# Attention and two expert layers on one core: other goals for the attention steps, another order of the first loads, later copies, GpSimd in program order

## The chip, the cores and the metric

The kernel runs on one core of a Trainium2 chip. The core has a matrix engine (TensorE, PE in the profile), a vector engine (VectorE, DVE), a scalar engine (ScalarE, ACT), a general engine (GpSimd, POOL) and an engine that does nothing here but issue transfers (SyncE, SP). Each engine takes its own instructions in order and waits for others at semaphores. Transfers (DMAs) are issued from SP, ScalarE or GpSimd and run on 16 DMA engines of the core. The metric is the time of one execution on the device in microseconds.

## The reference, cut to what matters

Shapes: 4 batches, 8 heads, 576 positions, head width 64; this makes 2304 tokens of width 512.

```python
# 1. attention with a decay per position, causal
scores = q @ k.T / 8 + cum[i] - cum[j]         # cum = cumsum(log(clip(f, 1e-4, 1)))
x = softmax(scores, causal) @ v                # then heads side by side: [2304, 512]
# 2. first layer: dense, 512 -> 2048 -> 512
h = x @ w_in
x = (h * clip(h + 3, 0, 6) / 6) @ w_out
# 3. second layer: each token goes to one of 8 experts, 512 -> 1024 -> 512
e = argmax(x @ w_gate)
out = softmax(x @ w_gate)[e] * sigmoid(x @ w_output_gate)[e] * (relu(x @ w1[e]) @ w2[e])
```

## The kernel before

All products are made from pairs of 16-bit numbers: each float32 matrix is split into a high part (float16) and a low part, and three matmuls stand for one.

**Opening.** The attention of the first batch runs ahead alone, while the weights of the first layer come in and are split. The function `attn_seq` (L635 on) is a generator that hands out attention in steps. Its prologue loads pieces of q and k (`load(i, "kq")`) and of v, computes the cumulative decay on VectorE (`decay`), stores it to DRAM (`store_decay`, L153) and reads it back in rows into K (`load_cum`, L215). The first two pieces of q and k are transposed on TensorE; their copies into the other half of K and Q are made on GpSimd (L249). Three steps end in the prologue; then each entry of a written list, `plan`, is one step: a unit of attention ("q" or "t": scores of a head, softmax, and the product with v of a unit some places back), a preparation of a piece of q and k ("p") or of v ("v"). Later pieces are transposed by DMA, and `copy_rows` copies the transposed rows to a second place (L260 on GpSimd for pieces 0 to 3, L262 on ScalarE for later ones). The copy is put into the order of instructions when the count that it starts with (`COPY_LAG`) has run out, one off at each unit, or when a unit needs it (`flush_for`).

Units wait in a list, `pend`, and `LAG = 4` of them are held back between scores and product. When the last unit of a group of row blocks has had its product, the group waits for two counts (`XLAG`), one at each unit, and then its rows are transposed into `xT` by DMA (`xtrans`, L561) and the group is `complete`. Preparations neither push a unit nor count. There are 12 groups, three for each batch; `ends[i]` is the place in the plan of the last unit of group i.

**Steps of the opening.** `pre_step` takes one attention step, then handles the weights: at the steps in `PRE_CONV` one piece of w_in is converted (three VectorE instructions L760 to L764, the high part on ScalarE L769, the low part on GpSimd L770), and one further piece of weights is loaded from SP (`load_next(nc.sync)`, L746). The prologue has loaded five pieces from ScalarE's queue already. The opening ends when the groups that chunk 0 needs are complete, and two more steps follow.

**Main part.** The first layer runs over 6 chunks of 384 tokens. `moe1_steps(c)` has 32 steps for a chunk: 16 of x @ w_in (12 matmuls each, L803) and 16 of 12 matmuls of g @ w_out (L828). Between them attention steps are put in by pace: the loop has a goal for the chunk, `goals[c]`, a number of attention steps, and takes steps so that the goal is reached at 0.9 of the chunk's steps (0.75 in chunk 4). After the chunk's last step, a loop takes attention steps one after another until the groups that the next chunk needs are complete. When all of attention is done, `open_weights` gives its memory to the expert weights, whose loads and conversions are then spread over the following steps.

**What sets the order.** TensorE, ScalarE and VectorE run in program order in the opening and the main part (`manual_schedule`), SP in the opening's first part only. Elsewhere SP and GpSimd are ordered by a planner, which simulates the program and issues what it takes to be ready first. `issue_after` puts instructions behind a given one on its engine; `gate` holds the transposes into `xT` of the third block of the first batch.

The parts that the change touches, with the line numbers of the profile:

Of the kernel before, what the change touches and what calls it, by code (L numbers as in the profile page):

```python
# [33 lines left out]

GATE_LOAD = 8

COPY_LAG = 1

LEAD = 2

LAG = 4

XLAG = 2
# [19 lines left out]
def attention_moe_kernel(ctx: ExitStack, tc: tile.TileContext, q, k, v, f, w_in, w_out,  # L63
# [7 lines left out]
    NTB = 5  # L71
# [184 lines left out]
    def copy_rows(i, out, in_):  # L256

        def go():
            if i < SPARE_PIECES:
                nc.gpsimd.tensor_copy(out=out, in_=in_)  # L260
            else:
                nc.scalar.activation(out=out, in_=in_, func=AF.Copy)  # L262
        copies.append([COPY_LAG, i, go])

    def flush_copies(due):
        for x in [x for x in copies if due(x)]:
# [368 lines left out]
    def attn_seq():  # L635

        def drain(n):
            while len(pend) > (min(n, EARLY_LAG) if pend and first_units(pend[0]) else n):
                pv(pend.pop(0))

        def step(u):
            todo, behind[:] = behind[:], []
            for f_ in todo:
                f_()
            if u:
                flush_for(u)
                score(u)
            turns, unturned[:] = unturned[:], []
            while unsoft:
                soft(unsoft.pop(0))  # L650
            for x in turns:
                turn(x)
            while outs:
                outs.pop(0)()
            if u:
                unsoft.append(u)
                pend.append(u)

        def after(n):
            drain(n)  # L660
            finish(1)
            for x in copies:
                x[0] -= 1
            flush_copies(lambda x: x[0] < 0)

        unsoft = []
        setup_ident()
        cp = decay()
        nc.scalar.activation(out=ap1.tile([P, 4], F32, tag="nm", name="warm", bufs=4)[:, 0:1], in_=bias3, func=AF.Exp)
        for i in range(4):  # L670
            load(i, "kq")
        for i in range(2):
            load(i, "v")
        setup()
        store_decay(cp)
        for hh in range(2):
            load_cum(0, hh)
        load(2, "v")
        banks.extend([(ps_mm, "mm")] * 3 + [(ps_sc, "sc")] * 2 + [(ps_pv, "pv")] * 2 + [(ps_mm, "mm")])
        for i in range(PE_PIECES):  # L680
            prep_k(i)
            load_next(nc.scalar)
            prep_q(i)
            load_next(nc.scalar)
        while behind:
            behind.pop(0)()
        prep(0, 2, "k")
        load_next(nc.scalar)
        yield "end"
        prep_v(0, 0)  # L690
        yield "end"
        prep(0, 2, "q")
        prep_v(0, 1)
        yield "end"
        for it in plan:
            if it is None:
                step(None)
                after(LAG)
            elif it[0] == "p":
                if it[2] == 4 or it[2] < 2 and it[1]:  # L700
                    load_cum(it[1], min(it[2], 2))
                if it[1:] == (0, 3):
                    for _ in range(3):
                        load_ahead()
                prep(it[1], it[2])
            elif it[0] == "v":
                prep_v(it[1], it[2])
            else:
                step(it)
                yield "mid"  # L710
                after(LAG)
            yield "end"
        step(None)
        for n in range(LAG, -1, -1):
            after(n)
            yield "end"
            step(None)
        while late:
            finish(1)
            yield "end"  # L720
# [484 lines left out]
        if loads and (loads[0][0] == "wi" or nsteps[0] >= WO_STEP) and len(loads) > 2 * NF - EARLY_LOADS:  # L1205
            load_next(nc.sync)

    with tc.manual_schedule(engines={mybir.EngineType.SP}):
        while len(complete) < need[0]:
            pre_step()  # L1210
    for _ in range(LEAD):
# [1 line left out]
    held = False  # L1213
    EARLY_CONV_DONE = 2 * NF - len(conv)
    assert len(conv) == len(CONV_AT), (len(conv), nsteps)
    goals = [ends[need[c + 1] - 1] + 1 + LAG + XLAG for c in range(NCH - 1)]
    mp2 = None
    px_ctx = ctx.enter_context(ExitStack())
    iota = None
# [17 lines left out]
    for c in range(NCH):  # L1237
# [14 lines left out]
        for part in moe1_steps(c):  # L1252
            k_ += part == "end"
            now = k_ + (part == "mid")
            share = min(1.0, now / pace)
            if c == 0:
                share = F1_SHARE * now / NF if now < NF else F1_SHARE + (1 - F1_SHARE) * min(1.0, (now - NF) / (pace - NF))
            want = start + (goal - start) * share
            if part == "mid":
                held = nsteps[0] < want and adv_part() == "mid"  # L1260
                continue
            if held:
                adv_part()
                held = False
            while nsteps[0] < want and adv():
                pass
            for split in late_steps:
                split()
                load_next(nc.scalar)
            late_steps.clear()  # L1270
            for lo in wlo:
                lo()
            wlo.clear()
            if c == 0 and k_ == GATE_LOAD:
                load_gates()
            if conv and k_ == CONV_AT[2 * NF - EARLY_CONV_DONE - len(conv)]:
                assert conv[0] not in loads
                late_steps.append(conv_raw(*conv.pop(0), later=True))
            elif not conv and mp2 is None:
                stage_ctx.close()  # L1280
                mp2 = moe1_ctx.enter_context(tc.tile_pool(name="mp2", bufs=1))
                ps_x = px_ctx.enter_context(tc.tile_pool(name="ps_x", bufs=1, space=PSUM))
                setup_gates()
            if gq and k_ in (3, 4, 6, 7, 8, 9):
                run(gq[0])
                if k_ == 9:
                    gq.pop(0)
            if c == NCH - 2 and wp is None and len(complete) == 3 * B:
                open_weights()
            if wg_ and nw < 4 * KD + 1 and (c < NCH - 1 or k_ % 4 == 0 or k_ > NF and k_ % 4 != 1):  # L1290
                run(wg_)
                nw += 1
            if c == NCH - 1 and k_ > 14:
                for i in [rq.pop(0) for _ in range(min(2, len(rq)))]:
                    rank_onehot(R0, i, 0, P)
                    rank_onehot(R, i, P, CAP)
                    if i == NBL - 1:
                        reserve()
                        table(R0, 0, const, ps_mm, (0,), NBL)
                        for e in range(2):  # L1300
                            row = wi[:, 0, 2 * e]
                            gather(e, (0,), (row[:, 0:2 * DM].rearrange("p (a b) -> p a b", b=P),
                                                   row[:, 2 * DM:4 * DM]))
                            h_tile(e, (0,), wi[:, 0, 2 * e + 1].rearrange("p (a c b) -> p a c b", c=2, b=P))
# [123 lines left out]
```

## Time and profile before

| | us |
|---|---|
| median of 3 runs (lowest to highest) | 887.76 (887.01 to 891.34) |
| the profiled execution | 883.18 |
| its span in the profile | 881.5 |
| PE busy | 733.6 |
| ACT, DVE, POOL busy | 456.8, 454.1, 317.4 |

A profile comes from one execution. The page sums up each engine; a view of stretches gives the busy time of each engine between two moments; a view in order of time gives single instructions, with the idle time of their engine before them and what ended it. The granted clock of TensorE has two levels here, 1.2 and 2.4 GHz, shown as 0.5 and 1.0.

### The profile page before, as it was taken

The page shows a single profiled execution, that of the slowest core. Times are in us where ns is not written, and L with a number is a line of the kernel's source. Part 1 is how long each engine was busy: PE and PEld are TensorE (multiplying, and loading weights), DVE is VectorE, ACT ScalarE, POOL GpSimd, SP SyncE. Part 2 cuts the span into 40 slices and gives each one's busy share as a digit, 9 for nine tenths or more (in the row PEclk, how much of TensorE's full clock was granted, in tenths as well). Part 3 has the DMA queues.
Part 4 walks back from the last instruction along what each step waited for, and adds up shares of the span by engine and source line. Part 5 has one row for each costly group of instructions (what it writes and reads, how often), then busy time and mean ns, then how long its engine had stood idle before and what let it go on. Part 6 is the DMA issues. An engine that isn't in the chain of part 4 may idle for free. (4 is left out here: it accounts for less than half of the span.)

```text
span 881.5 us, 16560 instructions
## 1 busy us (share of the span) xinstructions
PE 733.6 (83%) x6142; PEld 481.3 (55%) x6153; DVE 454.1 (52%) x1254; ACT 456.8 (52%) x904; POOL 317.4 (36%) x402
## 2 busy tenths in 40 slices
PE   2456879749998499959896699969989999999994
PEld 2344546425565266626564366646567776666762
DVE  7687688635743065217642285127853456646520
ACT  5557577645765377327774376125442445545430
POOL 9566446562344334323454234110103421321010
PEclk7576899988999699969998799989999999999997
DMA  9994559984466846355685434250688679989300
GB/s 249 253 252 90 119 85 209 231 168 91 71 130 106 169 82 118 64 110 107 101 156 125 95 65 92 26 162 29 211 219 203 176 233 324 295 190 251 139 36 26
DMA packets 268066, 129.00 MB, mean 146 GB/s; under 512 B 218946, under 2 KB 251810, under 8 KB 267972
## 3 DMA queue, kind: packets, MB, share of 16 engines
q1 hardware_dynamic: 254564, 103.66, 54.2%
q0 software_dynamic: 4960, 15.73, 5.2%
q10 hardware_dynamic: 8448, 8.39, 3.1%
q8 instruction: 54, 0.88, 0.4%
q14 instruction: 40, 0.33, 0.1%
HBM read 71.52 MB, written 10.08 MB: 93 GB/s over the span
## 5 line engine op out<-in xcount | busy, mean ns | idle before, releaser
L803 PE MATMUL mm<-xT,wi 128*128 128x384 f16 x912 | 169.8, 344 | 60.4 <-DMA xT<-xn 55.9
L828 PE MATMUL mm<-g,wo 128*128 128x384 f16 (+1 forms) x1152 | 195.2, 328 | 0.3 <-POOL wo L770 0.3
L803 PEld LDWEIGHTS <-wi 128*128 128x128 f16 (+1 forms) x1152 | 113.3, 101 | 137.6 <-DMA xT<-xn 44.5
L828 PEld LDWEIGHTS <-wo 128*128 128x128 f16 (+1 forms) x1152 | 110.7, 98 | 71.4 <-issue 1.5
L457 POOL TENSOR_TENSOR pn<-ms,pn 128x384 bf16<-128x384 f32 (+1 forms) x80 | 80.7, 1010 | 143.0 <-ACT pn L456 112.7
L1113 PEld LDWEIGHTS <-W 128*128 128x128 f16 (+1 forms) x1344 | 101.0, 99 | 9.1 <-issue 0.6
L1113 PE MATMUL mm<-g,W 128*128 128x256 f16 (+3 forms) x1152 | 96.6, 246 | 0.5 <-DVE wo L1117 0.5
L811 DVE SCALAR_TENSOR_TENSOR mm<-hr,mm 128x384 f32<-128x384 f32 x76 | 42.5, 560 | 104.3 <-ACT hr L810 103.8
L1132 PE MATMUL mm<-W,wo 128*128 128x512 f16 (+1 forms) x422 | 94.0, 379 | 1.1
L448 ACT ACTIVATE ms<-ms,nm 128x512 f32<-128x512 f32 (+3 forms) x144 | 79.8, 576 | 7.7 <-DVE nm L389 6.6
L1004 DVE TENSOR_TENSOR W<-stw,W 128x1024 bf16<-128x1024 f32 x46 | 55.4, 1222 | 46.1 <-ACT W L1001 45.9
L810 ACT ACTIVATE hr<-mm,bias 128x384 f32<-128x384 f32 x76 | 43.9, 578 | 67.5 <-PE mm L803 67.4
L389 DVE CUSTOM_DVE_ANT_1 ms<-sc,mask 128x128 f32<-128x128 f32 (+3 forms) x128 | 59.3, 486 | 29.8 <-PE sc L344 29.2
L1132 PEld LDWEIGHTS <-wo 128*128 128x128 f16 (+1 forms) x432 | 41.8, 98 | 50.7 <-ACT W L1001 1.2
L1139 POOL DMA_INDIRECT out_dram<-wo,ids x18 | 21.4, 1190 | 118.5 <-ACT wo L1138 95.3
L493 PE MATMUL pv<-vt,pt 128*128 128x65 f16 x320 | 42.1, 199 | 19.7 <-ACT pt L442 10.2
L1117 DVE SCALAR_TENSOR_TENSOR wo<-mm,wo 128x128 bf16<-128x128 f32 (+1 forms) x96 | 33.3, 356 | 47.2 <-ACT wo L1116 44.7
L344 PE MATMUL sc<-K,q 128*128 128x128 f16 (+2 forms) x192 | 49.8, 318 | 9.2 <-DVE nm L389 4.8
L344 PE MATMUL sc<-K,Q 67*128 67x128 f16 (+2 forms) x192 | 49.8, 316 | 8.6 <-DMA K<-cumd 8.6
L838 DVE SCALAR_TENSOR_TENSOR x<-mm,x 128x384 bf16<-128x384 f32 x24 | 13.4, 558 | 84.5 <-ACT x L837 80.0
L1001 ACT ACTIVATE W<-stw 128x1024 f16<-128x1024 f32 x46 | 47.5, 1049 | 16.6 <-DMA stw<-in_moe_w_dram 16.5
L816 DVE TENSOR_TENSOR g<-mm,g 128x384 bf16<-128x384 f32 x76 | 42.2, 556 | 22.5 <-ACT g L813 21.8
(213 smaller groups left out, 1220.1 us busy)
## 6 DMA issues: line engine op xcount, KB each, us to landing
stw<-in_moe_w_dram SPq DMA_DIRECT2D x46, 512.0 KB, 4.7
stx<-in_moe_w_dram SPq DMA_DIRECT2D x18, 512.0 KB, 5.4
wo<-in_moe_w_in_dram SPq DMA_DIRECT2D x11, 512.0 KB, 6.1
raw<-in_moe_w_out_dram ACTq DMA_DIRECT2D x11, 512.0 KB, 4.5
rows<-rw POOLq DMA_DIRECT2D x15, 256.0 KB, 3.2
ld<-in_v_dram SPq DMA_DIRECT2D x13, 256.0 KB, 3.8
ld<-in_k_dram SPq DMA_DIRECT2D x12, 256.0 KB, 3.1
ld<-in_q_dram SPq DMA_DIRECT2D x12, 256.0 KB, 3.1
```

The costliest lines, as they stand in the source:

```text
L344: nc.tensor.matmul(po, lhsT=lhs[0:rows], rhs=r if n > 1 else r[:, :, 0], start=x == 0, stop=x == 1)
L389: nc.vector.tensor_tensor_reduce(out=pairs(ms[:, off:off + w]), in0=ps[:, 0:w].rearrange("p (c j) -> p c j", c=2), in1=pairs(mask[:, 640 - ...
L448: nc.scalar.activation(out=ms[:, off:off + w], in_=ms[:, off:off + w], func=AF.Exp, scale=-1.0, bias=nm[:, i:i + 1])
L457: nc.gpsimd.tensor_tensor(out=lo.bitcast(BF16), in0=ms[:, 0:N], in1=hi, op=ALU.subtract)
L803: nc.tensor.matmul(ps[:, 0:w], lhsT=l.bitcast(BF16) if a else l, rhs=r.bitcast(BF16) if b2 else r, start=i == 0, stop=i == 3 * KD - 1)
L810: nc.scalar.activation(out=hr, in_=pw, func=AF.Relu, bias=bias3)
L811: nc.vector.scalar_tensor_tensor(out=pw, in0=hr, scalar=6.0, in1=pw, op0=ALU.min, op1=ALU.mult)
L828: nc.tensor.matmul(ps[:, 0:w], lhsT=l.bitcast(BF16) if a else l, rhs=r.bitcast(BF16) if b2 else r, start=i == 0, stop=i == 3 * NF - 1)
L1001: nc.scalar.activation(out=hi, in_=sts[i], func=AF.Copy)
L1004: nc.vector.tensor_tensor(out=lo.bitcast(BF16), in0=st, in1=hi, op=ALU.subtract)
L1113: nc.tensor.matmul(ps[:, 0:w], lhsT=l.bitcast(BF16) if a else l, rhs=r.bitcast(BF16) if b2 else r, start=i == 0, stop=i == 3 * KD - 1)
L1132: nc.tensor.matmul(ps, lhsT=l.bitcast(BF16) if a else l, rhs=r.bitcast(BF16) if b2 else r, start=i == 0, stop=i == 3 * NF2 - 1)
```

## The change

- The goals of the chunks become four steps higher.
- In the prologue three pieces of q and k are loaded first, then one of v; the second piece of v and the fourth of q and k come behind the store and the reading back of the decay, the third piece of v behind the preparation of K's third piece. Two pieces of weights instead of five are loaded from ScalarE's queue there, after the transposes on TensorE.
- The copies of pieces 0 to 4 start with a count of 5 instead of 1.
- In the opening's first part GpSimd, too, runs in program order.
- The two loads of gate weights are put behind the last transpose in `gate`.

```diff
-COPY_LAG = 1
+COPY_LAG, EARLY_COPY = 1, 5
...
-        copies.append([COPY_LAG, i, go])
+        copies.append([EARLY_COPY if i < NTB else COPY_LAG, i, go])
...
-        for i in range(4):
+        for i in range(3):
             load(i, "kq")
-        for i in range(2):
-            load(i, "v")
+        load(0, "v")
         setup()
         store_decay(cp)
         for hh in range(2):
             load_cum(0, hh)
-        load(2, "v")
+        load(1, "v")
+        load(3, "kq")
...
             prep_k(i)
-            load_next(nc.scalar)
             prep_q(i)
-            load_next(nc.scalar)
         while behind:
             behind.pop(0)()
+        load_next(nc.scalar)
+        load_next(nc.scalar)
         prep(0, 2, "k")
-        load_next(nc.scalar)
+        load(2, "v")
...
-    with tc.manual_schedule(engines={mybir.EngineType.SP}):
+    with tc.manual_schedule(engines={mybir.EngineType.SP, mybir.EngineType.Pool}):
         while len(complete) < need[0]:
             pre_step()
...
-    goals = [ends[need[c + 1] - 1] + 1 + LAG + XLAG for c in range(NCH - 1)]
+    goals = [ends[need[c + 1] - 1] + 5 + LAG + XLAG for c in range(NCH - 1)]
...
             if c == 0 and k_ == GATE_LOAD:
-                load_gates()
+                with tc.issue_after(gate[-1]):
+                    load_gates()
```

## Rows read from the trace of the kernel before

**Rows 1.** The page: busy time of the engines; busy DMA share in 40 slices.
```profile
PE 733.6 (83%) x6142; PEld 481.3 (55%) x6153; DVE 454.1 (52%) x1254; ACT 456.8 (52%) x904; POOL 317.4 (36%) x402
...
DMA  9994559984466846355685434250688679989300
```
**Rows 2.** Stretches: us; busy PE, PEld, DVE, ACT, POOL; clock, DMA share, GB/s.
```profile
0.00:90.30 90.30, 41.75 (x344) 32.24 (x345) 65.07 (x160) 51.66 (x100) 62.52 (x104) 0.68 0.86 209
90.30:200.00 109.70, 83.79 (x670) 52.55 (x670) 71.19 (x184) 69.30 (x140) 60.26 (x69) 0.92 0.76 162
```
**Rows 3.** Order of time, PE: first matmuls of chunks 1 to 5 (start, us, idle before).
```profile
199.98 5.78 PE L803 MATMUL mm<-xT,wi 128*128 128x384 f16 x24 [12.61 <-DMA xT<-xn]
...
300.10 4.02 PE L803 MATMUL mm<-xT,wi 128*128 128x384 f16 x12 [6.84 <-DMA xT<-xn]
...
389.68 4.02 PE L803 MATMUL mm<-xT,wi 128*128 128x384 f16 x12 [10.69 <-DMA xT<-xn]
...
493.45 5.82 PE L803 MATMUL mm<-xT,wi 128*128 128x384 f16 x24 [14.53 <-DMA xT<-xn]
...
582.45 7.64 PE L803 MATMUL mm<-xT,wi 128*128 128x384 f16 x36 [7.68 <-DMA xT<-xn]
```
**Rows 4.** The same: first attention matmul behind four chunks; twelve matmuls at full clock.
```profile
184.05 0.27 PE L344 MATMUL sc<-K,q 128*128 128x256 f16 x1
...
206.21 2.11 PE L803 MATMUL mm<-xT,wi 128*128 128x384 f16 x12
...
281.62 0.22 PE L344 MATMUL sc<-K,q 128*128 128x128 f16 x1
...
377.32 0.38 PE L344 MATMUL sc<-K,q 128*128 128x512 f16 x1
...
573.43 0.19 PE L491 MATMUL pv<-vt,pt 128*128 128x65 f16 x1
```
**Rows 5.** The same, PE and SP's queue, ahead of chunk 1.
```profile
186.88 0.22 PE L344 MATMUL sc<-K,Q 67*128 67x128 f16 x1
...
195.79 2.62 SPq L561 DMA_TRANSPOSE xT<-xn  x2
```
**Rows 6.** The same, PE ahead of chunk 2.
```profile
290.10 0.21 PE L492 MATMUL pv<-vt,pt 128*128 128x64 bf16 x1 [3.35 <-POOL vt L362]
```
**Rows 7.** The same, the opening: SP's queue, PE and DVE.
```profile
9.48 3.04 SPq L860 DMA_DIRECT2D wg<-in_moe_w_gate_dram  x1
12.56 0.51 SPq L861 DMA_DIRECT2D wg<-n_moe_w_output_gate_dram  x1
13.20 1.25 SPq L153 DMA_DIRECT2D cumd<-cp  x1
20.82 0.59 SPq L215 DMA_DIRECT2D K<-cumd  x2
...
22.50 0.27 PE L344 MATMUL sc<-K,Q 67*128 67x128 f16 x1 [8.62 <-DMA K<-cumd]
...
23.23 0.29 DVE L389 CUSTOM_DVE_ANT_1 ms<-sc,mask 128x128 f32<-128x128 f32 x1 [1.26 <-PE sc L344]
```
**Rows 8.** The same, the opening's copies; the last line from PE's waits, 60 to 72.
```profile
31.86 1.03 POOL L260 COPY K<-K 64x1024 f16<-64x1024 f16 x1 [8.56 <-DMA K<-kp]
...
34.04 0.69 DVE L764 SCALAR_TENSOR_TENSOR w<-wo,cv 128x512 int32<-128x512 int32 x1 [5.93 <-POOL wi L770]
...
53.48 0.42 DVE L516 TENSOR_TENSOR xs<-pv,rl 128x256 f32<-128x256 f32 x1 [2.03 <-POOL xn L524]
...
PE pv L493 <- ACT pt L442: 4.7, 1, 4.7
```
**Rows 9.** Stretches of the opening (columns as in rows 2).
```profile
9.00:12.00 3.00, 1.44 (x12) 0.90 (x9) 2.94 (x5) 1.07 (x2) 2.78 (x9) 1.00 1.16 312
...
36.00:40.00 4.00, 1.78 (x16) 1.48 (x14) 3.50 (x6) 3.57 (x9) 3.92 (x5) 0.50 1.10 351
```
**Rows 10.** The page's transfers: KB of one, median us from issue to landing.
```profile
wo<-in_moe_w_in_dram SPq DMA_DIRECT2D x11, 512.0 KB, 6.1
```

## The prediction

> **What bounds the kernel now.** I read the page first, then the stretches cut at the first matmul of each chunk, then the order of time around those cuts. The page says that TensorE is the busiest engine by far, 733.6 us of 881.5 [rows 1], so the question is where its missing 148 us lie. The stretches give two places [rows 2]. The opening, up to 90.3 us, holds 41.75 us of matmuls in 90.3: there VectorE is the fullest engine (65.07 us), and it stands still behind others. Chunk 0, up to 200.0, has 83.79 of 109.7, and most of the lost 25.9 us is one hole at its end.
>
> The order of time shows that hole at every chunk boundary: the first matmul of chunks 1 to 5 comes after waits of 12.61, 6.84, 10.69, 14.53 and 7.68 us for the transposes that bring x into xT, 52.35 us in all [rows 3]. In front of each hole stand attention steps, after the last feed-forward matmul of the chunk (from 184.05, 281.62, 377.32 and 573.43 on, four of the five, [rows 4]). So attention is late there, by a few steps at each boundary.
>
> The code tells how late. The counter of steps is at 3 before the plan begins, and a step for plan entry i leaves it at i+4. A group of row blocks is transposed once five more units have been pushed after its last one (four are held back, and the second of two counts comes one unit later). Preparations ("p", "v") are steps too, but push nothing. Counting along the plan, the steps that the next chunk needs are 58, 85, 106, 134 and 157; the goals are 54, 79, 104, 130 and 154. So 4, 6, 2, 4 and 3 steps are left when the chunk's matmuls end, and they run in a bunch with nothing beside them.
>
> **The change part by part.**
>
> *Goals four steps on.* They become 58, 83, 108, 134 and 158, so 0, 2, 0, 0 and 0 steps are left. By the pacing rule the needed step is done at feed-forward step 28, 26, 28 and 23 of 32 at boundaries 1, 3, 4 and 5. A step of 12 matmuls is 2.11 us at the full clock [rows 4], so at boundaries 1 and 4 at least 4 x 2.11 = 8.4 us of matmuls follow the last needed step, and two more attention steps lie between it and the last matmul that x depends on. Today that stretch, from the last attention matmul at 186.88 to the first of chunk 1 at 199.98 with the issue of the transposes at 195.79 [rows 5], is 13.1 us with four steps bunched. Two paced steps of about 2.5 us (one feed-forward step of 2.11 us and an attention step's own matmuls, an estimate) and 8.4 us make 13.4, so what stays there is about 0, and I take 1.5 us each; by the other end it is 13.1 - 8.4 = 4.7. Boundaries 3 and 5 have 12 and 19 us of cover, so 0 stays. At boundary 2 two steps stay, the second half of a V preparation and one unit, and the rows that x needs are still normalised in the bunch. The nearest row is boundary 3 of now, where two steps are left: from 377.32 to 389.68, 12.4 us, against 300.10 - 281.62 = 18.5 us now [rows 3, 4], which has a wait for V of 3.35 us in it [rows 6]. I take 18.5 - 12.4 = 6.1 saved. Sum: (12.6 - 1.5) + 6.1 + 10.7 + (14.5 - 1.5) + 7.7 = 48.6 us.
>
> *The clock behind a hole.* After these waits matmuls run at the lower of two levels first: 24 in 5.78 us, 12 in 4.02, 24 in 5.82, 36 in 7.64 [rows 3], against 2.11 for 12 at the full one. Without the hole 1.6 + 1.9 + 1.6 + 1.3 = 6.4 us come back at boundaries 1, 3, 4 and 5; boundary 2 keeps its loss.
>
> *What the moved steps cost where they go.* The number of steps over the chunks hardly changes (27, 27, 23, 26, 24 against 27, 27, 21, 28, 23), and their matmuls are the same. But in chunk 0 four steps move in among matmuls, beside the last weight conversions. Outside the boundary TensorE loses 25.9 - 12.6 = 13.3 us there [rows 2, 3], 0.5 us for each of 27 steps. Four more by that price are 2 us. The ends are 0 (the steps merely fill) and 13.3 (the chunk's other waits double). I take 4 us for all chunks. In chunk 4 attention ends at step 23, so expert weights are fetched and converted beside feed-forward steps there instead of in chunk 5. TensorE waits for none of it now; I cost it at 0, hidden behind 9 steps of 2.11 us.
>
> *The opening.* Three edits act on it. First the order of loads: piece 3 and the second V come behind the store of the cumulative decay, three of five early weight loads leave ScalarE's queue, and the gate weights, whose issue holds SP from 9.48 just ahead of that store (13.20) [rows 7], go behind the first x transposes. The store can go at about 9.5, where its data are ready; TensorE's wait of 8.62 us for it, until 22.50 [rows 7], shrinks. But the first unit's reduction on VectorE (23.23) has three weight conversions ahead of it in program order, and the third load is now issued on SP behind the decay and four loads. From the store at 9.5, the 7.6 us until its reload as now [rows 7], five issues of 0.51, 6.1 to land [rows 10] and 2.1 of conversion (three of 0.69) make 27.8, so 4.5 us late; with a store that lands in 3 us and a load in 4 it would be in time. I take 3 us late.
>
> Second, the copies of transposed rows wait for five units to pass instead of one. Now GpSimd reaches the copy at once and stands 8.56 us for the transpose; behind it wait the weights' low halves, so VectorE stands 5.93 us, and later 2.03 us behind the second copy; the copy on ScalarE holds the probabilities for which TensorE waits 4.7 us [rows 8]. The copies come before the unit that needs them in either case, so 5.9 + 2.0 + 4.7 = 12.6 us go. Late next are the weights: loads go one per step, one to four steps ahead of their conversion, and the DMA engines are full for the first 66 us (the first three of 40 slices, 22 us each, at 9, [rows 1]). I charge 1.6 us for that. Third, GpSimd in program order: its instructions have the same durations, and with the copies out of the way none stands long; 0.
>
> Net of the opening: -12.6 + 3 + 1.6 = -8 us. Its ends: -21.2 (the 8.6 us wait goes too, nothing is late) and +4.5 (the three waits come back at other places).
>
> A rule that speaks against the order of loads: the Trainium skill ("Trainium Kernel Development and Optimization", Key Constraints) says that DMAs from all queues share the same 16 engines, so issuing from several saves only issue time. The trace agrees: SP's queue alone moved 351 GB/s between 36 and 40 us, both queues together 312 between 9 and 12 [rows 9]. By that rule the three loads lose no bandwidth by leaving ScalarE; were the queues additive, three loads of 512 KB at 312 GB/s, 5 us, would be lost, and the sum would be 829 instead of 824.
>
> *Sum* against the profiled execution's own 883.2 us: 883.2 - 48.6 - 6.4 + 4 - 8 = 824.2. The median of the runs shown lies 4.6 us above that execution; I add 1 of it and forecast **825 us**.
>
> **The rivals.**
> - *Chain as long as today.* SP and GpSimd are in the planner's order in the main part, and x could again be queued behind other transposes. Then 4.7 us stay at boundaries 1 and 4 instead of 1.5, the clock falls there again (3.2 us), and boundary 2 saves nothing (6.1): 824 + 6.4 + 3.2 + 6.1 = 840. For it: between the last matmul at 186.88 and the transposes at 195.79 lie 8.9 us [rows 5]. Against: eight microseconds of matmuls lie beside them now. Chance 0.2.
> - *The opening gives nothing or loses,* first weights too late: 825 + 8 to 825 + 12.5, 833 to 838. For it: saturated transfers. Chance 0.14.
> - *Both of these, or crowded chunks* (the 13.3 end): about 850. Chance 0.07.
> - *The goals don't do what they say,* because waits only move to the paced steps: only the opening is won, 875. Against: outside the holes TensorE is nearly full. Chance 0.03.
> - *Slower: each weight conversion of the opening waits for its load.* VectorE takes them in order, and every unit queues behind. One landing is 6.1 us [rows 10]; 14 such loads are 85 us, which makes 883.2 - 51 + 85 = 917. It decides against the change from 51/14 = 3.6 us per load on. Now the loads are five to eight ahead and no conversion waits; against it, the loads stay one to four steps of about 3 us ahead. Chance 0.04.
> - *More than forecast* (the opening's better end, 806 to 812): 0.07.
>
> **How the numbers follow.** The forecast with its own range of 814 to 832 has 0.45. The range of 806 to 850 takes in the openings of either end, the longer chain and most of the crowded case; about 0.15 lies outside. About 0.5% is what a measurement of this kernel can tell from no change. All cases but the slower one, and a part of the waits-only-move case, end below 883: faster 0.94, the same 0.02, slower 0.04.
>
> **What would show it.** In the trace after: waits of the first matmul for xT below 2 us at boundaries 1, 3, 4 and 5, and some 8 to 12 us at boundary 2 with an attention unit ahead of it; no half-rate matmuls behind the others; the first chunk starting at 78 to 86 us; no GpSimd copy standing for a transpose. It is wrong if xT waits stay above 5 us at three boundaries, if VectorE stands for weight loads by over 10 us in the opening, or if chunk 0 has over 20 us of idle TensorE.

## The result and the profile after

The changed kernel takes 835.98 us (median of 4 runs, 835.23 to 837.45), the kernel before 887.38 (885.51 to 891.34) beside it: a ratio of 0.9417 [0.9382, 0.9452], or 51 us less. The forecast was 825, the range 806 to 850. The profiled execution took 837.45 us, 45.7 less than that of before; the sum was made for a difference of 59. That pair is the longest execution of the changed kernel beside a short one of the kernel before (883.18, below the lowest of the four): by the medians 7.6 us of the 59 are missing, by the profiled pair 13.

First the page of the changed kernel, which answers to [rows 1]: busy time of the engines.

```profile
PE 734.7 (88%) x6153; PEld 481.4 (58%) x6153; DVE 454.8 (54%) x1254; ACT 454.5 (54%) x904; POOL 314.8 (38%) x402
```

The engines are as busy as they were, within 3 us each: the work is the same, and what changed is idle time. TensorE's share rises from 83 to 88%.

Where the idle time went is read from the first matmul of each chunk, in order of time on TensorE (start, us, idle before), against [rows 3]; the first line here is chunk 0:

```profile
82.42 4.02 PE L803 MATMUL mm<-xT,wi 128*128 128x384 f16 x12 [4.14 <-DMA xT<-xn]
...
190.38 6.73 PE L803 MATMUL mm<-xT,wi 128*128 128x384 f16 x24 [3.85 <-DMA xT<-xn]
...
284.77 3.67 PE L803 MATMUL mm<-xT,wi 128*128 128x384 f16 x12 [8.55 <-DMA xT<-xn]
...
363.96 2.11 PE L803 MATMUL mm<-xT,wi 128*128 128x384 f16 x12
...
450.60 4.07 PE L803 MATMUL mm<-xT,wi 128*128 128x384 f16 x24 [0.28 <-DMA xT<-xn]
...
532.06 4.06 PE L803 MATMUL mm<-xT,wi 128*128 128x384 f16 x24
```

The waits at boundaries 1 to 5 are now 3.85, 8.55, 0, 0.28 and 0, together 12.7 where they were 52.35. Behind boundaries 3, 4 and 5 the matmuls run at the full clock at once; behind 1 and 2 the first ones still run at half. At boundary 2 the wait for xT alone is longer than before, but the bunch of attention steps ahead of it is shorter: from its first matmul (273.52) to chunk 2 it is 11.3 us, against 18.5.

These starts cut the execution into stages (chunk 5 ends at the first expert matmul, 649.70 before and 604.79 after). In the forecast's row, the boundary's wait is put into the chunk that it ends, the clock into the next, and the 4 us for moved steps into chunk 0:

| us | opening | chunk 0 | 1 | 2 | 3 | 4 | 5 | experts |
|---|---|---|---|---|---|---|---|---|
| before | 90.3 | 109.6 | 100.1 | 89.6 | 103.8 | 89.0 | 67.2 | 231.8 |
| after | 82.4 | 108.0 | 94.4 | 79.2 | 86.6 | 81.5 | 72.7 | 230.9 |
| difference | -7.9 | -1.7 | -5.7 | -10.4 | -17.1 | -7.5 | +5.5 | -0.9 |
| forecast | -8.0 | -7.1 | -7.7 | -10.7 | -14.9 | -9.3 | -1.3 | 0 |

Two stages miss: chunk 0 by 5.4 us and chunk 5 by 6.8, together 12.2 of the some 13 missing. Each row is one execution. Chunk 0 took 109.6 to 112.2 us in the six profiles with goals of +1 (the kernel before and five of the table of experiments) and 105.9 to 108.9 in the six with +5 and the same conversions there, with means of 111.2 and 107.4: so 3.8 us are gained there by the means, and 1.7 in this pair, which leaves a miss of some 3 us instead of 5.4. Both misses show in the stretches of the changed kernel (us; busy PE, PEld, DVE, ACT, POOL; clock, DMA share, GB/s): opening, chunk 0 and chunk 5.

```profile
0.00:82.42 82.42, 42.73 (x344) 32.05 (x344) 64.92 (x160) 51.33 (x100) 63.41 (x104) 0.65 0.99 229
82.42:190.38 107.96, 87.97 (x669) 54.22 (x670) 73.76 (x184) 69.17 (x140) 58.88 (x67) 0.91 0.78 155
532.06:604.79 72.73, 67.11 (x443) 39.91 (x442) 42.38 (x114) 28.51 (x49) 3.68 (x5) 0.95 0.50 145
```

**Chunk 0.** TensorE's 669 matmuls take 87.97 us where they took 83.77 (90.34 to 199.97), and the waits inside the chunk are longer. These are TensorE's waits from 82.42 to 190.37 in the changed kernel (total, times, longest):

```profile
PE sc L409 <- DVE nm L389: 5.3, 1, 5.3
PE pv L491 <- DMA pt<-pn: 4.3, 2, 3.0
PE mm L803 <- DMA xT<-xn: 4.1, 1, 4.1
PE pv L492 <- POOL vt L362: 2.4, 2, 1.3
PE pv L491 <- ACT vt L361: 1.7, 1, 1.7
PE mm L803 <- DVE g L816: 1.2, 1, 1.2
PE sc L344 <- DVE nm L415: 1.1, 1, 1.1
```

The same view of the kernel before (90.34 to 199.97):

```profile
PE mm L803 <- DMA xT<-xn: 3.6, 1, 3.6
PE mm L803 <- DVE g L816: 3.1, 4, 1.1
PE sc L344 <- DVE nm L389: 3.0, 2, 1.8
PE sc L409 <- DVE nm L389: 2.9, 1, 2.9
PE pv L492 <- POOL vt L362: 2.2, 2, 1.1
PE pv L491 <- DMA pt<-pn: 1.7, 1, 1.7
...
```

Without the xT lines, which are the chunk's start, these are 16.0 us against 13.4 (with two waits of 0.3 and 0.2). So 8.8 us came off the boundary's wait, 2.6 were added to waits inside and 4.2 to the matmuls' own time: 2.0 are left, and 1.7 were measured.

The matmuls' own time grew mostly by the clock. In order of time on TensorE in the changed kernel, behind two of these waits:

```profile
114.72 0.27 PE L409 MATMUL sc<-K1t,q 128*64 128x64 f16 x2 [5.33 <-DVE nm L389]
...
115.63 8.52 PE L803 MATMUL mm<-xT,wi 128*128 128x384 f16 x36
...
167.15 0.20 PE L491 MATMUL pv<-vt,pt 128*128 128x65 f16 x1 [2.98 <-DMA pt<-pn]
...
167.43 2.99 PE L828 MATMUL mm<-g,wo 128*128 128x384 f16 x12
```

At the full clock 36 such matmuls take 6.01 us and 12 take 2.11, so these two places hold some 3.4 of the 4.2 us. The same two waits were 2.92 and 1.69 us in the kernel before, and no half-rate matmuls followed them.

The longest of the waits, 5.33 us for VectorE's maxima (L389), leads back to ScalarE. These rows of ScalarE and VectorE stand ahead of it:

```profile
106.64 1.06 ACT L262 ACTIVATE Q<-q 64x1024 f16<-64x1024 f16 x1 [0.94 <-DMA q<-qp]
...
108.85 0.56 DVE L811 SCALAR_TENSOR_TENSOR mm<-hr,mm 128x384 f32<-128x384 f32 x1 [3.51 <-ACT hr L810]
```

VectorE stands 3.51 us for an evacuation (L810), which in ScalarE's order comes behind two copies of transposed rows (L262), the second of which waits for its transpose. Only then follow the three instructions of a weight conversion, some short ones and the maxima. In the kernel before the same copy waited for nothing, and VectorE waited 0.72 us there.

**Chunk 5.** Attention now ends before the last steps of chunk 4, so expert weights are opened there. In order of time on ScalarE in the changed kernel, around the start of chunk 5 (532.06):

```profile
522.61 2.17 ACT L1001 ACTIVATE W<-stw 128x1024 f16<-128x1024 f32 x2 [5.46 <-DMA stw<-in_moe_w_dram]
...
537.17 1.06 ACT L1001 ACTIVATE W<-stw 128x1024 f16<-128x1024 f32 x1 [1.16 <-DMA stw<-in_moe_w_dram]
538.13 0.47 ACT L837 ACTIVATE x<-mm 128x384 f16<-128x384 f32 x1
```

and on TensorE:

```profile
539.25 2.76 PE L803 MATMUL mm<-xT,wi 128*128 128x384 f16 x12 [3.13 <-DVE x L838]
```

Almost every conversion (L1001) of that stretch waits for its load, and the evacuation of chunk 4's last outputs (L837) stands behind one in ScalarE's order. TensorE needs the buffer that L837 and L838 empty: 3.13 us lost at 539.25 and a stretch at a mean clock of 0.95 instead of 0.98.

**Opening.** The waits of [rows 7, 8] are gone or changed places. TensorE's first decay wait falls from 8.62 to 1.6 us (its waits, 0 to 90), but a wait for VectorE's maxima comes in:

```profile
PE sc L344 <- DVE nm L389: 8.4, 1, 8.4
...
PE sc L344 <- DMA K<-cumd: 1.6, 1, 1.6
```

because in VectorE's order a weight conversion stands ahead of them, and its load is late (order of time on VectorE):

```profile
22.49 0.69 DVE L760 TENSOR_SCALAR cv<-wo 128x512 int32<-128x512 int32 x1 [3.22 <-DMA wo<-in_moe_w_in_dram]
...
24.62 0.28 DVE L389 CUSTOM_DVE_ANT_1 ms<-sc,mask 128x128 f32<-128x128 f32 x1
```

### The profile page after: what moved, and what is told of

Its sections match the earlier page's. It is cut to its first block, busy times and chain, and to the rows that moved or that the text cites. A ratio compares the mean times of both kernels' runs of the same rounds, so it can differ in the third digit from the quotient of the medians.

```text
span 835.7 us, 16571 instructions
## 1 busy us (share of the span) xinstructions
PE 734.7 (88%) x6153; PEld 481.4 (58%) x6153; DVE 454.8 (54%) x1254; ACT 454.5 (54%) x904; POOL 314.8 (38%) x402
## 5 line engine op out<-in xcount | busy, mean ns | idle before, releaser
L828 PE MATMUL mm<-g,wo 128*128 128x384 f16 (+1 forms) x1152 | 197.4, 329 | 0.0
L803 PE MATMUL mm<-xT,wi 128*128 128x384 f16 x912 | 167.6, 340 | 21.2 <-DMA xT<-xn 16.8
L457 POOL TENSOR_TENSOR pn<-ms,pn 128x384 bf16<-128x384 f32 (+1 forms) x80 | 80.8, 1012 | 105.1 <-ACT pn L456 83.9
L1113 PEld LDWEIGHTS <-W 128*128 128x128 f16 (+1 forms) x1344 | 101.5, 99 | 12.6 <-issue 4.2
L1113 PE MATMUL mm<-g,W 128*128 128x256 f16 (+3 forms) x1152 | 98.3, 248 | 3.8 <-DMA g<-g 3.3
L448 ACT ACTIVATE ms<-ms,nm 128x512 f32<-128x512 f32 (+3 forms) x144 | 79.9, 577 | 9.8 <-DVE nm L389 6.4
L811 DVE SCALAR_TENSOR_TENSOR mm<-hr,mm 128x384 f32<-128x384 f32 x76 | 42.5, 559 | 61.2 <-ACT hr L810 60.9
L389 DVE CUSTOM_DVE_ANT_1 ms<-sc,mask 128x128 f32<-128x128 f32 (+3 forms) x128 | 59.5, 486 | 24.6 <-PE sc L344 19.9
L810 ACT ACTIVATE hr<-mm,bias 128x384 f32<-128x384 f32 x76 | 43.8, 576 | 41.2 <-PE mm L803 40.7
L1139 POOL DMA_INDIRECT out_dram<-wo,ids x18 | 19.0, 1055 | 123.1 <-ACT wo L1138 101.3
L838 DVE SCALAR_TENSOR_TENSOR x<-mm,x 128x384 bf16<-128x384 f32 x24 | 13.4, 557 | 86.4 <-ACT x L837 86.4
L1116 ACT ACTIVATE wo<-mm 128x128 f16<-128x128 f32 (+1 forms) x96 | 31.5, 331 | 44.6 <-PE mm L1113 40.9
L1001 ACT ACTIVATE W<-stw 128x1024 f16<-128x1024 f32 x46 | 47.5, 1049 | 14.6 <-DMA stw<-in_moe_w_dram 14.4
L491 PE MATMUL pv<-vt,pt 128*128 128x65 f16 x320 | 43.9, 202 | 9.0 <-DMA pt<-pn 6.7
```

What stands on the lines that cost most here:

```text
L389: nc.vector.tensor_tensor_reduce(out=pairs(ms[:, off:off + w]), in0=ps[:, 0:w].rearrange("p (c j) -> p c j", c=2), in1=pairs(mask[:, 640 - ...
L448: nc.scalar.activation(out=ms[:, off:off + w], in_=ms[:, off:off + w], func=AF.Exp, scale=-1.0, bias=nm[:, i:i + 1])
L457: nc.gpsimd.tensor_tensor(out=lo.bitcast(BF16), in0=ms[:, 0:N], in1=hi, op=ALU.subtract)
L491: nc.tensor.matmul(oc, lhsT=pt[:, g, :], rhs=V[:, kb, h, 0:65], start=kb == 0, stop=False)
L803: nc.tensor.matmul(ps[:, 0:w], lhsT=l.bitcast(BF16) if a else l, rhs=r.bitcast(BF16) if b2 else r, start=i == 0, stop=i == 3 * KD - 1)
L810: nc.scalar.activation(out=hr, in_=pw, func=AF.Relu, bias=bias3)
```

## The experiments

The theory is the forecast's with two terms re-sized: the goals win what the boundaries lost, and lose in chunk 0 (its steps are slow wherever they stand) and in chunk 5 (expert weights come too early); the opening adds its 8 us. Times are medians; each ratio is to runs of the kernel before on the same chip.

| us | time | ratio | opening | 0 | 1 | 2 | 3 | 4 | 5 | experts |
|---|---|---|---|---|---|---|---|---|---|---|
| goals alone | 845.41 | 0.9488 [0.9433, 0.9544] | 90.0 | 108.9 | 95.6 | 79.9 | 86.2 | 82.0 | 73.0 | 230.0 |
| opening alone | 880.42 | 0.9918 [0.9892, 0.9944] | 83.0 | 110.3 | 101.4 | 88.8 | 102.9 | 88.7 | 67.0 | 235.6 |
| weights at chunk 5 | 837.04 | 0.9428 [0.9384, 0.9472] | 83.2 | 107.6 | 96.0 | 79.1 | 86.4 | 81.4 | 65.6 | 233.9 |
| goals +9 | 836.43 | 0.9432 [0.9376, 0.9487] | 83.8 | 111.1 | 89.3 | 83.4 | 85.3 | 81.7 | 70.8 | 225.9 |
| copies alone | 889.50 | 0.9986 [0.9956, 1.0016] | 89.4 | 111.4 | 101.3 | 88.2 | 102.6 | 88.8 | 67.1 | 243.2 |
| loads alone | 886.85 | 0.9950 [0.9916, 0.9984] | 85.3 | 111.9 | 100.3 | 89.3 | 103.4 | 88.9 | 67.2 | 240.1 |
| gate split moved | 835.33 | 0.9372 [0.9325, 0.9419] | 83.3 | 107.9 | 96.4 | 80.3 | 85.6 | 81.3 | 70.1 | 230.2 |
| weights at every third step | 832.00 | 0.9323 [0.9275, 0.9372] | 83.5 | 106.3 | 97.0 | 80.7 | 86.7 | 81.4 | 65.8 | 230.5 |
| GpSimd's order alone | 889.94 | 0.9996 [0.9957, 1.0036] | 92.0 | 112.1 | 101.1 | 87.8 | 102.9 | 88.7 | 67.2 | 235.2 |
| order and copies | 882.55 | 0.9910 [0.9872, 0.9948] | 82.2 | 112.2 | 101.4 | 87.7 | 103.1 | 88.7 | 67.1 | 235.3 |
| best version | 824.29 | 0.9233 [0.9188, 0.9279] | 83.9 | 105.9 | 86.6 | 79.7 | 86.9 | 81.4 | 65.8 | 232.7 |

The stages come from one profiled execution each. The expert part lies between 225.9 and 243.2 us among these, though most of them change nothing there; so small effects are read from a stage, and the total decides only where the interval lets it.

**Goals alone** (the kernel before with the higher goals and nothing else).

```diff
-    goals = [ends[need[c + 1] - 1] + 1 + LAG + XLAG for c in range(NCH - 1)]
+    goals = [ends[need[c + 1] - 1] + 5 + LAG + XLAG for c in range(NCH - 1)]
```

> The kernel before with the goals four steps higher and nothing else of the change. Theory (the parts add up): between the first matmuls of chunks 0 and 5 and on to the end the change saved 1.7 + 5.7 + 10.4 + 17.1 + 7.5 - 5.5 + 0.9 = 37.8 us; the goals alone give that, 887.4 - 37.8 = 849.6 us, ratio 0.957, and the first matmul of chunk 0 stays at 90 us. Rival (the opening's order has a part in the later savings, through the transfers that it leaves over): above 858 us.

845.41 us, some 4 less than the theory's 849.6 (its ratio of 0.957 lies just outside the interval). Chunks 0 to 5 are those of the changed kernel within 1.2 us, chunk 5's loss included, and the opening is that of before: some 43 us of the 51 are the goals'.

**Opening alone** (the changed kernel with `+ 1` again in the goals).

```diff
-    goals = [ends[need[c + 1] - 1] + 5 + LAG + XLAG for c in range(NCH - 1)]
+    goals = [ends[need[c + 1] - 1] + 1 + LAG + XLAG for c in range(NCH - 1)]
```

> The changed kernel with the goals of before: only the opening is changed. Theory (the parts add up): the 7.9 us of the opening alone, 879.5 us, ratio 0.991, with waits for xT of about 52 us in all as before. Rival (an earlier start only makes a later wait longer, since something else sets the boundary): 885 to 888 us.

880.42 us, opening 83.0, chunks 1 to 5 as before. The two ratios multiply to 0.941; the whole has 0.9417. Within their intervals the parts add.

**Weights at chunk 5** (the changed kernel; the opening of the expert weights waits for chunk 5).

```diff
-            if c == NCH - 2 and wp is None and len(complete) == 3 * B:
+            if False and c == NCH - 2 and wp is None and len(complete) == 3 * B:
```

> The changed kernel, but the memory of attention is handed to the expert weights only at the start of chunk 5, as happened before the change. Theory (chunk 5 is 5.5 us longer since the high parts on ScalarE, which wait for their loads, stand ahead of the last evacuations of chunk 4, so that the third group of matmuls of chunk 5 waits 3.1 us and the clock falls): 836 - 5.5 = 830.5 us, ratio to the kernel before 0.936, chunk 5 to its first expert matmul in 67 us as before. Rival (the weights done early are worth something at the expert layers, or chunk 5 is long for another reason): 836 us or more.

Chunk 5 falls from 72.7 to 65.6 us, so the early weights are its cause; the total doesn't move, as the rival had it. In the profiled execution 3.0 of the 7.1 us come back behind it, where TensorE waits for what chunk 5 leaves late. Its waits from 605 on:

```profile
PE mm L927 <- DVE oh L916: 2.9, 1, 2.9
```

In the changed kernel that row isn't there, and the longest is another:

```profile
PE mm L1113 <- DMA g<-g: 3.3, 1, 3.3
```

The interval of the total (0.5% to either side) hides what is left.

**Goals +9** (the changed kernel, goals four steps higher still).

```diff
-    goals = [ends[need[c + 1] - 1] + 5 + LAG + XLAG for c in range(NCH - 1)]
+    goals = [ends[need[c + 1] - 1] + 9 + LAG + XLAG for c in range(NCH - 1)]
```

> The changed kernel with the goals four steps higher again (eight above those of before). Theory (the waits for xT that are left at boundaries 1 and 2, 3.9 and 8.6 us, are attention late by its chain): both go, and about 4 us of half clock with them, 836 - 16 = 820 us. Rival (chunk 0 is full on VectorE and ScalarE; steps that move into it make their waits there): boundary 2 saves 10 us, chunk 0 gives back 5 or more, 830 us or above.

No wait for xT is left at boundaries 1 to 5, and the time is the same, where the theory had 820 us: the rival held. Chunk 1 wins 5.1 us, chunks 0 and 2 give back 3.1 and 4.2. With +9 chunk 0 is as long as with +1 (111.1 us against 109.6 to 112.2), though its boundary has no wait left: what the boundary gives, the chunk's inside takes.

**Copies alone** and **GpSimd's order alone** (each in the kernel before).

```diff
+COPY_LAG, EARLY_COPY = 1, 5
...
-        copies.append([COPY_LAG, i, go])
+        copies.append([EARLY_COPY if i < NTB else COPY_LAG, i, go])
```

> The kernel before with only the later copies (count 5 instead of 1 for pieces 0 to 4). Theory (the copies are what the opening gains from: VectorE's 5.9 and 2.0 us and TensorE's 4.7 us go, less what becomes late next): the first matmul of chunk 0 at 79 to 83 us instead of 90.3, 877 to 881 us, ratio 0.988 to 0.993. Rival (the order of loads carries the gain): above 885 us.

```diff
-    with tc.manual_schedule(engines={mybir.EngineType.SP}):
+    with tc.manual_schedule(engines={mybir.EngineType.SP, mybir.EngineType.Pool}):
```

> Only GpSimd's program order is added to the kernel before (copies keep their count of 1, loads and goals as before). Theory: in program order the copies stand where the count puts them, one unit after the transpose, so GpSimd still reaches them at once and stands for the transposes as before (14 to 15 us in two waits); opening 89 to 91 us, ratio to the kernel before 0.997 to 1.003. Rival: program order alone puts the weights' low halves ahead of the copies and carries the 3 us of the opening that the loads don't: opening 86 to 88 us, ratio 0.996 or less.

Neither moves the time: openings of 89.4 and 92.0 us. GpSimd's waits from 0 to 90 show why. The wait for the copy of K is 13.9 us in the kernel before; with the copies alone:

```profile
POOL K L260 <- DMA K<-kp: 14.8, 2, 9.7
```

With its program order alone:

```profile
POOL K L260 <- DMA K<-kp: 13.2, 2, 7.8
```

While the planner orders GpSimd, the later count doesn't bind it; in program order with a count of 1 the copy stands where it stood. For the first the theory fell; for the second it held in time and waits, with an opening 1 us longer than named.

**Order and copies** (both diffs together, loads and goals as before).

> The count of 5 for the copies and GpSimd's program order are both added to the kernel before, loads and goals as before. Theory: the count only works where the order of GpSimd follows it; together the 8.6 us wait of GpSimd for the transpose goes, VectorE's 5.9 us behind it too, and the opening ends 3 to 8 us earlier (82 to 87 us); ratio 0.991 to 0.997. Rival: the opening is bound by the order of loads alone, and without it the copies' waits come back at other places: opening 89 to 91 us, ratio 0.997 to 1.003.

The theory held: the opening falls by 8.1 us to 82.2, at least as much as with the load order beside it (82.4 to 83.9 in the seven profiles with the whole opening). GpSimd's copy of K is gone from its waits (0 to 90), which now begin with weights:

```profile
POOL wi L770 <- ACT wi L769: 9.9, 5, 5.6
...
POOL Q L260 <- DMA q<-qp: 0.5, 1, 0.5
```

TensorE still waits for the decay here:

```profile
PE sc L344 <- DMA K<-cumd: 9.1, 1, 9.1
```

**Loads alone** (the kernel before with the order of the first loads and the gate loads' place).

```diff
-        for i in range(4):
+        for i in range(3):
             load(i, "kq")
-        for i in range(2):
-            load(i, "v")
+        load(0, "v")
...
-                load_gates()
+                with tc.issue_after(gate[-1]):
+                    load_gates()
```

> The kernel before with only the other order of the first loads and the gate loads put behind. Theory (TensorE's wait for the decay shrinks from 8.6 us, but VectorE then waits some 3 us for the third weight load, so that the first unit starts no sooner, and the copies stand in the way as before): chunk 0 starts at 89 to 93 us, 886 to 891 us. Rival (the order of loads carries the gain): chunk 0 at 82 to 85 us, 879 to 882 us.

The opening falls by 5.0 us to 85.3, between theory and rival. Loads win 5 without the copies and nothing beside them, in single profiles: the two don't add.

**Gate split moved** (the changed kernel). In chunk 0 VectorE's split of the gate weights (L865) takes 3.10 us in the changed kernel and 0.23 in the kernel before, ahead of boundary 1.

```diff
-        nc.vector.tensor_copy(out=wg[:, 0], in_=wg32)
-        nc.vector.tensor_tensor(out=wg[:, 1].bitcast(BF16), in0=wg32, in1=wg[:, 0], op=ALU.subtract)
...
+            if c == 1 and k_ == 1 and part == "end":
+                nc.vector.tensor_copy(out=wg[:, 0], in_=wg32)
+                nc.vector.tensor_tensor(out=wg[:, 1].bitcast(BF16), in0=wg32, in1=wg[:, 0], op=ALU.subtract)
```

> The changed kernel with the two VectorE instructions that split the gate weights moved from the end of chunk 0 to the first step of chunk 1. Theory (one of them took 3.10 us in the changed kernel instead of 0.23, in the chain from the last product to the transposes that chunk 1 waits for): the wait of 3.85 us at boundary 1 falls below 1.5 us and no half clock follows, 836 - 5 = 831 us. Rival (boundary 1 waits by SP's queue and GpSimd; the instruction ran long beside a wait): the wait stays at 3 to 4 us, 836 us.

Moved, it takes 0.23 us; the wait at boundary 1 is 3.40 instead of 3.85, and chunk 0 is 107.9 us as before the move. The theory fell. That instruction isn't what chunk 0 lost.

**One VectorE instruction for each conversion** (the changed kernel; w_in and w_out are other matrices of like size, as the same edit also acts on the 16 conversions of the opening).

```diff
+        if later:
+            nc.vector.tensor_scalar(out=t, in0=w[:, :, 1], scalar1=-0x03000001, scalar2=0,
+                                    op0=ALU.bitwise_and, op1=ALU.bitwise_or)
+        else:
...
```

> The changed kernel, in which the 16 weight conversions of chunk 0 take one VectorE instruction instead of three (the bits are only masked, so w_out is another matrix of like size, and what follows chunk 0, the routing of tokens above all, differs). It takes 32 instructions of 0.69 us, 22 us, out of VectorE's order in chunk 0 and leaves all loads, ScalarE's and GpSimd's halves and the attention steps. Only the length of chunk 0 is to be read. Theory: chunk 0 gained 1.7 us instead of 7 because the four steps moved into it stand behind the conversions in VectorE's order; without these the waits for VectorE's maxima (5.3 and 1.1 us) go with their slower matmuls, and chunk 0 is 98 to 103 us instead of 108. Rival: the steps are late by their own chain of engines and transfers (waits for pt and vt of 8.4 us), and chunk 0 stays at 105 to 109 us.

Chunk 0 is 105.1 us. (The total, one execution of 864.65 us with another routing of the tokens, can't be compared with the others.) Its stretch:

```profile
79.42:184.55 105.13, 85.86 (x669) 53.47 (x670) 51.28 (x152) 68.48 (x140) 59.62 (x67) 0.92 0.82 158
```

and its longest wait on TensorE:

```profile
PE sc L409 <- DVE nm L389: 5.6, 1, 5.6
```

VectorE has 22.5 us less to do, and the chunk is 2.8 shorter, at the rival's edge. The wait for the maxima didn't go: it isn't the conversions that hold it. The conversions carry some 3 us, as far as one profile tells. Ahead of that wait stands the copy on ScalarE again (in this kernel L814 and L815 are what L810 and L811 are above):

```profile
103.79 1.05 ACT L262 ACTIVATE Q<-q 64x1024 f16<-64x1024 f16 x1 [3.11 <-DMA q<-qp]
...
106.00 0.56 DVE L815 SCALAR_TENSOR_TENSOR mm<-hr,mm 128x384 f32<-128x384 f32 x1 [6.14 <-ACT hr L814]
```

So a rival is left that the rows speak for: ScalarE's copies of the later pieces, which keep the count of 1 in the changed kernel. No run moved them.

**Weights at every third step** (the changed kernel).

```diff
-            if wg_ and nw < 4 * KD + 1 and (c < NCH - 1 or k_ % 4 == 0 or k_ > NF and k_ % 4 != 1):
+            if wg_ and nw < 4 * KD + 1 and (k_ % 3 == 0 if c < NCH - 1 else k_ % 4 == 0 or k_ > NF and k_ % 4 != 1):
```

> The changed kernel with one conversion of expert weights in every third step of chunk 4 instead of every one (three there instead of nine, the rest in chunk 5 and behind). Theory (ScalarE's conversions wait 5.5 us for their first load and then stand one behind another ahead of the last evacuations): chunk 5 to its first expert matmul takes 67 us instead of 72.7, and the expert layers keep the 231 us of the changed kernel, 836 - 5.5 = 830.5 us. Rival (what chunk 5 gains the expert layers lose, as when the weights came late): 835 to 838 us.

The theory held: chunk 5 is 65.8 us and the expert part stays at 230.5. In order of time on ScalarE, near the end of chunk 4:

```profile
525.82 1.06 ACT L1001 ACTIVATE W<-stw 128x1024 f16<-128x1024 f32 x1 [5.10 <-DMA stw<-in_moe_w_dram]
528.03 0.49 ACT L837 ACTIVATE x<-mm 128x384 f16<-128x384 f32 x1 [1.15 <-PE mm L828]
528.42 1.05 ACT L1001 ACTIVATE W<-stw 128x1024 f16<-128x1024 f32 x1
```

The first conversion still waits 5.10 us for its load, but the evacuation behind it is not late: it waits for TensorE. The next conversion finds its load there. The stretch of chunk 5, to be read against the changed kernel's 72.73 at a clock of 0.95:

```profile
535.63:601.41 65.78, 64.57 (x444) 39.21 (x442) 43.48 (x115) 31.50 (x52) 4.72 (x5) 1.00 0.47 144
```

**Best version** (the kernel with weights at every third step, and two more steps in chunk 1's goal alone, which boundary 2 lacked).

```diff
-    goals = [ends[need[c + 1] - 1] + 5 + LAG + XLAG for c in range(NCH - 1)]
+    goals = [ends[need[c + 1] - 1] + (7 if c == 1 else 5) + LAG + XLAG for c in range(NCH - 1)]
```

> The changed kernel with the expert weights' conversions of chunk 4 at every third step only, and the goal of chunk 1 alone raised by two more steps. Theory: the wait of 8.55 us at boundary 2 goes as in the kernel with all goals at +9 (chunk 1 89 to 92 us instead of 94 to 97), without that kernel's losses in chunks 0 and 2 (108 and 80 us stay); about 827 us where the changed kernel is at 836, ratio to the kernel before 0.925 to 0.929. Rival: the steps that leave the boundary are paid in pace: chunk 2 or the waits inside chunk 1 grow by as much, ratio 0.931 to 0.935 as without the two steps.

824.29 us, ratio 0.9233 [0.9188, 0.9279], so better than both kernels, and a little better than the theory's 827, which the interval takes in. In order of time on TensorE, boundary 2:

```profile
276.41 2.12 PE L803 MATMUL mm<-xT,wi 128*128 128x384 f16 x12 [0.25 <-DMA xT<-xn]
```

Wait and half clock are gone, and chunk 1 is 86.6 us where it was 97.0 without the two steps. Chunk 2 pays nothing for it.

## Why the prediction was right or wrong

**What bounds the kernel: right.** The lost time lay in holes ahead of the chunks, and steps left over made them: the number of steps left after the change (0, 2, 0, 0, 0) and the waits (3.85, 8.55, 0, 0.28, 0) have their one large value at the same place, and two more steps there took it away.

**Goals: right at boundaries 2 to 5.** At boundary 2 the bunch became 7.2 us shorter, 6.1 were forecast. The waits forecast were 8 to 12 us at boundary 2, none at 3 and 5, 1.5 at 4. The clock came back at 3, 4 and 5, as forecast. At boundary 1 the forecast took 1.5 us between ends of 0 and 4.7; 3.85 were measured, and its clock was not won back: the rival of a chain as long as today was right there, and only there.

**Moved steps in chunk 0: the term was mis-sized.** The forecast had 4 us with an upper end of 13.3. Of the 8.8 us that came off boundary 1, 1.7 arrived in the profiled pair, so the moved steps cost 7.1; by the means of six profiles on either side 3.8 arrived and they cost some 5. The forecast took the price of a step from the idle time and counted the clock at the boundaries only: longer waits inside the chunk were followed by matmuls at half clock (36 in 8.52 us instead of 6.01), which is most of the 4.2 us that the matmuls grew by. Idle TensorE in chunk 0, its last wait included, is 19.99 us, just under the 20 that were named as a sign of being wrong. Fewer conversions give back some 3 us, a short gate split or still higher goals nothing that shows. For the longest wait the rows lead to ScalarE's copies of transposed rows; that is read from traces and not tried, and what holds the other steps in chunk 0 stays open.

**Expert weights in chunk 4, costed at 0: the step that failed.** "TensorE waits for none of it now" was true of the kernel before, where these instructions stood elsewhere. Placed one per step, most of the conversions wait for their load on ScalarE, and the evacuation that TensorE needs stands behind one of them: chunk 5 grew by 5.5 us instead of shrinking by 1.3. The forecast named what is queued behind such a wait in the opening, but not here. With a conversion at every third step the whole of it came back.

**Opening: the sum right, its terms not all.** -8 was forecast, -7.9 measured, the better end of seven profiles of the whole opening (82.4 to 83.9 us). The copies were costed at -12.6 + 1.6 = -11 and won 8.1 together with GpSimd's program order; that order was costed at 0, but it is what lets the copies win anything. The load order was costed at +3 and measures 0.2 to 1.7 beside the copies. So that the sum came out is in part luck: two terms were too large, one either way. The first unit's maxima came 1.4 us later than before (24.62 against 23.23, [rows 7]), for the reason named, the third load. That it costs little at the end is seen in the opening without the load order (82.2 us): there the wait for the decay, 9.1 us, stands where the wait for the maxima, 8.4, stands here.

On the queues: the Trainium skill ("Trainium Kernel Development and Optimization", Key Constraints) has DMAs from all queues share the same engines. The runs don't speak against it: 229 GB/s over the opening with three weight loads moved to SP's queue and 229 (0.00 to 82.25) with all five on ScalarE's. But both openings move the same bytes in the same time, so this shows only that the move lost no bandwidth.

**Sum.** Chunk 0 by +5.4, chunk 5 by +6.8 and the rest by +1 make the 13 us by which the profiled execution gained less than the sum. By the medians 7.6 are missing, and chunk 5's 6.8 would be most of that. The time lies nearer to the rival's 840 than to 825, but by that rival's mechanism only at boundary 1.

## What to carry to other kernels

Count, along the written order, the steps that are left when a stage's matmuls end: that count named each hole here, and its size told which goal to raise and by how much. When work moves earlier, price what it pulls along behind it (here the expert weights): an instruction that waits for a transfer holds everything behind it on its engine, so space it by the time its transfer takes. A place in the written order binds only engines that follow that order; two edits that each do nothing may be one edit.

## What was not expected of the hardware

The same VectorE instruction (L865, 128x64) took 3.10 us in the profiles of five kernels, the changed one among them, and 0.22 to 0.23 in those of the other seven that have it at this line. In order of time on VectorE in the changed kernel:

```profile
179.53 3.10 DVE L865 TENSOR_TENSOR wg<-wg,wg 128x64 bf16<-128x64 f32 x1
```

Nothing is shown as awaited. On GpSimd in the same kernel, instructions stand back to back:

```profile
179.40 1.16 POOL L228 TENSOR_TENSOR qp<-ld,qp 64x512 f16<-64x512 f32 x1
180.51 1.17 POOL L770 TENSOR_TENSOR wo<-w,wo 128x512 bf16<-128x512 f32 x1
181.63 0.92 POOL L457 TENSOR_TENSOR pn<-ms,pn 128x384 bf16<-128x384 f32 x1
```

L865 begins inside the first and ends with the third (182.63 and 182.55). In the kernel before it began at 181.11, when one GpSimd instruction had ended (179.88 + 1.14) and the next had not begun (181.14), and took 0.23; in the six other short ones it also began while GpSimd stood still, in one of them (the copies alone) 0.04 us before GpSimd's next instruction. The Trainium skill ("SBUF — State Buffer", SBUF: two separate sides) says that a VectorE instruction with two inputs from SBUF, as L865 has, and a GpSimd instruction that reads SBUF contend for a shared pair of ports, an exclusive lock for the whole instruction. The rows agree, and go further: if this lock is the cause, L865 waited for three instructions in a row here, not one. That GpSimd is the cause wasn't tried by itself.

The clock fell inside a stage, too. In the changed kernel TensorE was busy for 0.17 us of the three from 164 to 167 us, at a granted clock of 1.00, and ran at 0.50 from 169 to 171 (stretches; columns as above):

```profile
164.00:167.00 3.00, 0.17 (x3) 0.00 (x0) 0.00 (x0) 1.18 (x2) 0.00 (x0) 1.00 1.22 299
169.00:171.00 2.00, 1.87 (x8) 0.87 (x7) 1.93 (x7) 1.84 (x5) 1.48 (x3) 0.50 0.33 116
```

Behind the hole of 0.28 us at boundary 4 no matmul was slow. The hole of 4.14 us ahead of chunk 0 tells nothing of this kind: the clock was at 0.50 before it (70 to 82 us).
